# Attention and an ELU network on one core: the network's layers and the attention's values on float16 pairs

## The chip, the core and the metric

The kernel runs on one core of a Trainium2 chip. The core has five engines that take their instructions from queues of their own: TensorE (PE; its weight loads are listed apart as PEld), VectorE (DVE), ScalarE (ACT), GpSimd (POOL) and SyncE (SP, which here only issues DMAs). They share an on-chip memory of 128 partitions (SBUF); matmuls write to an accumulation memory (PSUM) of banks of 512 float32 values per partition. The metric is the time of one execution on the device in microseconds, the median of the runs.

## What is computed

Eight batches of eight heads, 576 positions, head size 64, then a network of 4608 tokens from 512 to 2048 to 512. The attention has a causal mask and a bias from running sums of `s`:

```python
scores = scale * np.matmul(q, k.transpose(0, 1, 3, 2))
cum = np.cumsum(np.maximum(s, 0.0), axis=-1)
bias = -(cum[:, :, :, None] - cum[:, :, None, :])
scores = np.where(causal, -1000000000.0, scores + np.minimum(bias, 0.0))
attn = np.exp(scores - np.max(scores, axis=-1, keepdims=True))
attn = attn / (np.sum(attn, axis=-1, keepdims=True) + 1e-09)
x = np.matmul(attn, v)                      # heads side by side: 4608 x 512
h = x @ w_in                                # 512 -> 2048
g = np.where(h > 0.0, h, np.exp(np.minimum(h, 0.0)) - 1.0)
out = (g @ w_out).astype(np.float32)        # 2048 -> 512
```

All inputs are float32 but the two weight matrices, which arrive as float64; the kernel takes them as pairs of 32-bit words and puts a float32 together on the chip. The output has to be near float32 accuracy, so most products are split into parts.

## The kernel before

**A planner sets the order.** The code describes operations (`op`) with a priority, what they read and write, and one or more "ways": an engine, an assumed cost, and the instruction. `Plan.issue` repeatedly picks the operation and the way that can start first by these assumed costs (ties go to the lower priority number) and writes it into its engine's queue. Each engine then runs its queue in that fixed order, and waits where an operand isn't there. Many vector operations can go to DVE, ACT or POOL (`rounded`, `rest`, `psum_copy`, `halved`); those that read PSUM can't go to POOL. DMAs go into SP's queue in the same way.

**Attention.** A batch has four pairs `j` of heads. The first 320 positions of batches 0 to 2 are done by twelve "low" units on whole float32 operands (`prepare_low`, `scoring_low`, `weighing_low`). Then batches 3 to 7 follow in full, and at the end the "late" rest (256 positions) of batches 0 to 2; that makes 40 whole and 24 late units of one head each (`Unit`, `prepare`, `scoring`, `weighing`), and 20 small units for the first 64 positions of a pair. A unit loads q and k, splits them in two parts each, multiplies the scores (L882), adds the mask and takes the minimum (L885), exponentiates (L890), and makes from each probability block a float16 high and low part (`halved`, L929 to L943). DMA transposes them (`turned_load`, L369) into `T`. `weighing` multiplies them by the values: `values` loads v as float32 and forms remainders (`rest`, L387 and L388), whose upper 16 bits serve as three bfloat16 parts of v. Each of five key blocks takes three matmuls (L1013), the last takes two: two parts of v side by side, against the high part of the probabilities; the same against the low part; and the third part of v. `halves` (L1092, L1097) adds the two halves of the result into `x`, which goes to DRAM (`x_dram`).

**The network** goes over 12 chunks of 384 tokens (`moe_chunk`), in the order in which attention delivers rows: chunk 0 has batch 0's low rows and 64 of batch 1, chunk 2 ends with rows of batch 3, chunk 8 with rows of batch 7, chunk 11 with late rows of batch 2. A chunk loads `x` (`load_x`), splits it into `xh` and `xl` (a float32 rounded for TensorE's fast float32 form, "fp32r" in the profile, and its remainder), and goes over 16 slices f of 128 hidden values: `hidden(f)` multiplies, for four blocks c, high by high, high by low and low by high (L1178, 12 matmuls of 384 columns); ACT takes the exponential (L1186), ACT or DVE the part below zero (L1191 or L1195), DVE joins (L1200), ACT or DVE rounds into `gh` (L394), DVE forms `gl` (L1203); `project(f)` multiplies three blocks of 128 tokens in three parts each (L1216, 9 matmuls of 512 columns). `project(f-1)` stands behind `hidden(f)` in the queue. Chunks alternate with attention on PE from chunk 0 on.

**The weights.** `load_weights` loads 32 units (16 slices, two matrices) of 512 KB into buffers `io` (two; at first also two of `xx`, where `xh` and `xl` come later). Each is turned from float64 words into float32 by one ACT and two DVE operations (L544, L547, L550), then split by `rounded` and `rest` (L376 to L388) into `w_in_f[f]` or `w_out_f[f]`, which stay for the whole run. Their priority is `W0 + WD * f`, with WD 5, so they come between the low units. Until its first 60 us are over, the planner fills PE with scratch transposes (L1267).

Of the kernel before, what the change touches and what calls it, by code (L numbers as in the profile page):

```python
# [17 lines left out]
P = 128  # L18
# [6 lines left out]
N_ST, N_A, N_AV, N_H, N_IO, N_G, N_X, N_T, N_K = 2, 2, 1, 2, 2, 1, 1, 2, 1  # L25
# [6 lines left out]
W0, WD = 45, 5  # L32
# [3 lines left out]
N_HOME = 0  # L36


NATIVE, WHOLE = 0, 0
# [13 lines left out]
class Buf:  # L53


    def __init__(self, pool, shape, dtype, name, tag=None, bufs=1, others=()):
# [4 lines left out]
        self.others = [((id(pool), o[0]), *o[1:]) for o in others]  # L61
        self.tile = None
        self.parts = {}
        self.users = 0
        self.until = 0.0

# [11 lines left out]
class Plan:  # L78
# [32 lines left out]

    def op(self, prio, ways, reads=(), writes=(), late=()):
# [5 lines left out]
        for accesses, write in ((reads, False), (writes, True)):  # L118
            for a in accesses:
                b, part = a if isinstance(a, tuple) else (a, None)  # L120
                if not b.parts and b not in o.bufs:

                    n = self.tags.get(b.key, 0)
                    self.tags[b.key] = n + 1
                    o.new.append((b, n))
                    b.first = o
# [34 lines left out]
    def issue(self):  # L161
# [19 lines left out]
        while pending:  # L181
# [10 lines left out]
            for o in pending:  # L192
                t = 0.0
                for b, k in o.new:
# [4 lines left out]
                    if b.others and not busy:  # L199
# [77 lines left out]
def pe4(n):  # L277

    return 4 * pe(n)

# [35 lines left out]
def kernel(  # L316
# [66 lines left out]

    def rest(prio, n, dst, src, hi, reads, writes, only=None):
# [28 lines left out]
    vs = [plan.buf(const, [P, NQ + 1, 4, D], F32, f"vs_{k}") for k in range(2)]  # L413
# [110 lines left out]
    w_in_f, w_out_f = ([plan.buf(sb, [P, 2, 512], F32R, f"{n}_{f}") for f in range(NF)] for n in ("wi", "wo"))  # L524
    homes = [b.key[1] for pair in zip(w_in_f, w_out_f) for b in pair]
    wide = w_in.dtype != F32

    urgent = []

    def load_unit(f, kind, src, parts):  # L530

        prio = W0 + WD * f
        a, n = src.shape[1], f"{kind}{f}"
        later = homes[max(homes.index(parts.key[1]) + 1, len(homes) - N_HOME) :]
        shape, dtype = ([P, 512, 2], U32) if wide else ([P, 512], F32)
        raw = plan.buf(sb, shape, dtype, f"w_{n}", tag="io", bufs=N_IO,
                       others=[("xx", 2, 0)] + [(t, 1, 0) for t in later])
        if wide:
            load(prio, lambda: raw.v.rearrange("p (a n) t -> p a (n t)", a=a),
# [11 lines left out]
                raw.v[:, :, 0], raw.v[:, :, 1], 3, raw.v[:, :, 0],  # L551
                ALU.logical_shift_left, ALU.bitwise_or))], [(raw, 1)], [(raw, 0)])
            words = (raw, 0)
# [5 lines left out]
        def value():  # L559
            return raw.v[:, :, 0].bitcast(F32) if wide else raw.v  # L560
# [807 lines left out]
```

## Time and profile before

| what | value |
|---|---|
| time, median of 3 runs (lowest, highest) | 1125.65 us (1124.69, 1129.84) |
| the profiled execution: span from first to last instruction | 1121.7 us |
| median time less that span | 4.0 us |
| mean granted clock of TensorE | 1.000 |
| first matmul of the network | 87.15 us |
| last attention result stored | 968.88 us |
| DMA, mean over the span | 140 GB/s |

The profile lists for each engine the time in which it had an instruction running. Matmuls overlap on PE: the next one starts while the last one drains, so their durations add up to more than the time they take, and the distance of two starts is what one costs. "Idle before" is the time in which the engine had nothing running before an instruction, with whoever ended it. A granted clock of 1.00 is TensorE at full speed.

### The profile page before, as it was taken

The numbers are of one execution on the slowest core, as the hardware profiler recorded it, in microseconds if no ns is written. First come the engines' busy times: TensorE is split into PE (matmuls) and PEld (weight loads), VectorE is DVE, ScalarE is ACT, GpSimd is POOL, SyncE is SP. The second block draws the span as 40 slices with busy tenths as digits, with TensorE's granted clock in tenths as the row PEclk, the third lists the DMA queues.
The fourth block names the chain that finished last, engine by engine and source line by source line (L and its number), as shares of the span: only waits on it lengthen the run. The fifth ranks groups of instructions, "written<-read, shape, count | busy, mean of one in ns | idle before, by whom it ended". The sixth has DMA issues, their size and how long they took to land.

```text
span 1121.7 us, 19900 instructions
## 1 busy us (share of the span) xinstructions
PE 1098.8 (98%) x6069; PEld 955.5 (85%) x6069; DVE 842.3 (75%) x2133; ACT 627.1 (56%) x1525; POOL 448.5 (40%) x657
## 2 busy tenths in 40 slices
PE   8999999999999999999999999999999999999998
PEld 7779888888888888888888888888888888899997
DVE  6888999778888887677887887788888888422322
ACT  5887666455556655555565555555655556433433
POOL 7663573345436234344333533445444433100000
PEclk9999999999999999999999999999999999999999
DMA  6976788567666855666755656667787687210000
GB/s 171 274 196 203 183 206 191 124 141 167 154 127 143 175 126 127 153 141 139 158 117 122 162 136 138 145 131 177 167 185 165 138 191 144 51 57 1 29 1 28
DMA packets 341689, 156.52 MB, mean 140 GB/s; under 512 B 266424, under 2 KB 320464, under 8 KB 341584
## 3 DMA queue, kind: packets, MB, share of 16 engines
q1 hardware_dynamic: 341584, 155.27, 59.4%
q8 instruction: 48, 0.79, 0.3%
q14 instruction: 57, 0.47, 0.1%
HBM read 79.66 MB, written 19.32 MB: 88 GB/s over the span
## 4 chain that ended last, share of the span: by engine, by line
PE 73%; DVE 4%; DMA 3%; issue 1%; POOL 1%; ACT 1%; SPq 1%; POOLq 0%; DVEq 0%; ACTq 0%
PE o L1216 29%; PE h L1178 29%; PE av L1013 8%; PE sc L882 6%; DVE p L943 1%; DMA T<-p 1%; DMA stq<-in_qT_dram 1%; DVE p L885 1%; DMA q<-qs 0%; DMA vs<-in_vb_dram 0%; DVE h L1200 0%; DVE xl L387 0%; DMA out_dram<-ost 0%; DMA x_dram<-x 0%; DVE qs L387 0%
## 5 line engine op out<-in xcount | busy, mean ns | idle before, releaser
L1178 PE MATMUL h<-xh,wi 128*128 128x384 f32 x1536 | 444.6, 339 | 1.1 <-DVE gl L1203 1.1
L1216 PE MATMUL o<-wo,gh 128*128 128x512 f32 x1152 | 362.1, 395 | 0.1
L1178 PEld LDWEIGHTS h<-xh,wi 128*128 128x128 f32 x1536 | 282.6, 188 | 9.3 <-DVE gl L1203 2.4
L1178 PE MATMUL h<-xl,wi 128*128 128x384 f32 x768 | 258.4, 336 | 0.0
L1216 PEld LDWEIGHTS o<-wo,gh 128*128 128x128 f32 x1152 | 207.0, 188 | 27.4 <-DVE mn L885 0.5
L1216 PE MATMUL o<-wo,gl 128*128 128x512 f32 x576 | 227.3, 395 | 0.9 <-DVE gl L1203 0.9
L1200 DVE SCALAR_TENSOR_TENSOR h<-h,g 128x384 f32<-128x384 f32 x192 | 107.8, 561 | 121.6 <-ACT g L1191 120.1
L1186 ACT ACTIVATE g<-h 128x384 f32<-128x384 f32 x192 | 94.1, 490 | 175.4 <-PE h L1178 166.0
L890 ACT ACTIVATE p<-p,mn 128x192 f32<-128x192 f32 (+1 forms) x232 | 144.9, 625 | 72.2 <-DVE mn L885 69.1
L943 DVE SCALAR_TENSOR_TENSOR p<-p,sm,p 128x512 f16<-128x512 f32 (+3 forms) x239 | 170.6, 741 | 8.1 <-POOL p L935 4.9
L1178 PEld LDWEIGHTS h<-xl,wi 128*128 128x128 f32 x768 | 144.4, 188 | 6.8
L935 POOL TENSOR_SCALAR p<-p,sm 128x512 f16<-128x512 f32 (+3 forms) x125 | 87.8, 709 | 134.8 <-DVE sm L896 51.8
L394 ACT CAST gh<-h 128x384 fp32r<-128x384 f32 x175 | 83.5, 477 | 86.7 <-DVE h L1200 85.4
L1203 DVE TENSOR_TENSOR gl<-h,gh 128x384 fp32r<-128x384 f32 x192 | 105.8, 551 | 32.8 <-ACT gh L394 31.7
L1216 PEld LDWEIGHTS o<-wo,gl 128*128 128x128 f32 x576 | 108.0, 188 | 25.2 <-DVE gl L1203 1.3
L885 DVE CUSTOM_DVE_ANT_0 p<-sc,maskw 128x192 f32<-128x192 f32 (+1 forms) x232 | 109.7, 482 | 24.9 <-PE sc L882 21.1
L1013 PEld LDWEIGHTS <-vs 128*128 128x128 bf16 x896 | 79.7, 98 | 49.7 <-issue 13.9
L1013 PE MATMUL av<-T,vs 128*128 128x256 f16 (+5 forms) x896 | 119.2, 285 | 2.8 <-DMA T<-p 2.1
L388 POOL TENSOR_TENSOR vs<-vs 128x320 f32<-128x320 f32 x72 | 60.4, 839 | 124.6 <-DMA vs<-in_vb_dram 71.1
L882 PE MATMUL sc<-kh,qs 128*128 128x192 f32 (+2 forms) x272 | 87.2, 325 | 2.1 <-DVE mn L885 1.8
L882 PE MATMUL sc<-k,q 128*128 128x192 f32 (+2 forms) x272 | 83.8, 312 | 1.4 <-POOL k L388 0.9
L1191 ACT ACTIVATE g<-g 128x384 f32<-128x384 f32 x138 | 72.5, 525 | 4.2
(149 smaller groups left out, 1368.7 us busy)
## 6 DMA issues: line engine op xcount, KB each, us to landing
stk<-in_kT_dram SPq DMA_DIRECT2D x64, 288.0 KB
vs<-in_vb_dram SPq DMA_DIRECT2D x64, 160.0 KB
stq<-in_qT_dram SPq DMA_DIRECT2D x40, 256.0 KB
w_i<-in_w_in_dram SPq DMA_DIRECT2D x16, 512.0 KB
w_o<-in_w_out_dram SPq DMA_DIRECT2D x16, 512.0 KB
out_dram<-ost SPq DMA_DIRECT2D x32, 256.0 KB
x_dram<-x_None SPq DMA_DIRECT2D x20, 288.0 KB
q<-qs SPq DMA_DIRECT2D x40, 128.0 KB
```

Source lines behind the costliest of these rows:

```text
L394: ("ACT", act_c(n), lambda: act.copy(dst(), src())),
L882: pe_.matmul(view(sc.v[:, :cw]), l, r, start=n == 0, stop=n == len(pairs) - 1)
L885: op(prio, [("DVE", 84 + dve_p(cw), lambda i=i, sc=sc: dve.tensor_tensor_reduce(pt.v[:, i * cw : (i + 1) * cw], sc.v[:, :cw], mv(i * cw, c ...
L890: op(prio, [("ACT", 480 + w / 1.2, lambda: act.activation(pt.v[:, :w], pt.v[:, :w], AF.Exp, bias=mn.v[:, n - 1 : n], scale=-1.0, accum_out ...
L935: ("Pool", 160 + 1.04 * n, lambda part=part: pool.tensor_scalar(part(t16, 0), own(part), sm.v[:, r], 1.0, ALU.mult, ALU.mult)),
L943: ("DVE-SB", dve_2(n), lambda part=part: dve.scalar_tensor_tensor(part(t16, 1), own(part), sm.v[:, r], part(t16, 0), ALU.mult, ALU.subtract)),
L1013: op(prio, [("PE", cost, lambda m=m, operands=operands, rows=rows: pe_.matmul(av.v[:rows, dst], *operands(), start=first and m == 0, stop= ...
L1178: pe_.matmul(hp.v[:, :TC], w_in_f[f].v[:, part, c * P : (c + 1) * P], xx.v[:, c, :TC], start=(c == 0 and m == 0), stop=(c == NCB - 1 and m ...
L1186: op(side, [("ACT", act_c(TC), lambda: act.activation(g.v[:, :TC], hp.v[:, :TC], AF.Exp))], [hp], [g])
L1200: op(side, [("DVE", dve_p(TC), lambda: dve.scalar_tensor_tensor(hp.v[:, :TC], hp.v[:, :TC], 0.0, g.v[:, :TC], ALU.max, join[0]))], [g], [hp])
L1203: op(side, [("DVE", dve_p(TC), lambda: dve.tensor_tensor(gl.v[:, :TC], hp.v[:, :TC], gh.v[:, :TC].bitcast(F32), ALU.subtract))], [hp, gh], ...
L1216: pe_.matmul(acc[i].v, g.v[:, tb], w_out_f[f].v[:, part], start=(f == 0 and m == 0), stop=(f == NF - 1 and m == 2),)
```

## The change

All of it concerns in what form operands stand, and what has to be known before they can be made.

- **The network's chunks 1 to 11** multiply float16 pairs: `x`, `w_in`, the hidden values and `w_out` are each a float16 high part and a float16 remainder, after scaling by a power of two. The number of matmuls is the same. `hidden` now joins by a maximum in PSUM (`g` times the scale against `h`), and the pair `gg` is formed with a factor `2**-DOWN`; the scale is undone on the way out (`output`).
- **Chunk 0** (384 tokens) multiplies `x` and the weights as whole float32 (`hidden_native`, `project` with `native`): one product in place of three, no split. Its `x` is loaded straight into the buffers that `xh` and `xl` take later.
- **Scales** are found on chip: `peak` reduces each weight unit, each low unit's values and each group's values to one largest magnitude per partition. `scales_of` reduces these to one column, stores it to DRAM, loads it back in all partitions, reduces again and turns the exponent into a power of two. `x` is scaled by the scale of the values it comes from, since an average of values is no larger than the largest.
- **The weights** are kept as float32 (`w_all`) at first, are split into `w_parts` once all 32 are loaded and reduced (`weight_scales`, `split_unit`), and only the float16 parts are used after chunk 0. WD goes from 5 to 3; raw weights have the two `io` buffers alone.
- **The attention's values** of the 64 whole and late units are a scaled float16 pair. `group_values` loads a batch's values at once (four loads, placed 60 priority steps ahead), into the place of `w_parts[3]` for the first batch and of `w_all` for later ones; `pair_values` splits them. A key block takes two matmuls, both parts of v side by side, against the high and the low part of the probabilities; the last takes one.
- `kh` gets two buffers instead of one.

```diff
-N_ST, N_A, N_AV, N_H, N_IO, N_G, N_X, N_T, N_K = 2, 2, 1, 2, 2, 1, 1, 2, 1
+N_ST, N_A, N_AV, N_H, N_IO, N_G, N_X, N_T, N_K, N_V = 2, 2, 1, 2, 2, 1, 1, 2, 2, 2
+V_AHEAD = 60
-W0, WD = 45, 5
+W0, WD = 45, 3
...
+    def peak(prio, n, src, reads, at, axis=mybir.AxisListType.X, aside=None, also=()):
+        col = slice(at, at + 1)
+        ways = [("DVE-SB", 100 + 1.04 * n, lambda: dve.tensor_reduce(
+            peaks.v[:, col], src(), axis, ALU.max, apply_absolute_value=True))]
+        if aside is not None:
+            ways.append(("ACT", 480 + n / 1.2, lambda: act.activation(
+                aside(), src(), AF.Abs, accum_out=peaks.v[:, col])))
+        op(prio, ways, reads, [(peaks, at), *also])
...
+    def scales_of(prio, spans, dst):
...
+        def largest():
+            for m, (at, k) in enumerate(spans):
+                dve.tensor_reduce(own.v[:, m : m + 1], peaks.v[:, at : at + k], mybir.AxisListType.X, ALU.max)
+        def exponents():
+            dve.tensor_reduce(own.v, every.v.rearrange("p (n q) -> p n q", q=P), mybir.AxisListType.X, ALU.max)
+            bits = own.v.bitcast(U32)
+            dve.tensor_scalar(bits, bits, 23, 23, ALU.logical_shift_right, ALU.logical_shift_left)
+            power(scales.v.bitcast(U32)[:, dst : dst + n], bits, 2 * 127 + TOP)
...
+        op(prio, [("DVE-SB", 30.0 + 70 * n, largest)], used, [own])
+        load(prio, lambda: aside.v.rearrange("n p -> p n"), lambda: own.v, [own], [aside], P * n * 4)
+        load(prio, lambda: every.v, lambda: aside.v.rearrange("n p -> (n p)").partition_broadcast(P),
+             [aside], [every], P * P * n * 4)
+        op(prio, [("DVE-SB", 300.0 + 130 * n, exponents)], [every], [own, (scales, dst)])
...
+    def split_unit(f, kind):
...
+        scaled(prio, 512, high_v, value, lambda: scales.v[:, col], [place, (scales, 0)], [high])
+        op(prio, [("DVE-SB", dve_2(512), lambda: dve.scalar_tensor_tensor(
+            low_v(), value(), scales.v[:, col], high_v(), ALU.mult, ALU.subtract))],
+           [place, (scales, 0), high], [low])
...
+    def group_values(u):
+        at = groups.index((u.b, u.blocks[0] > 0))
+        prio, first, col = u.prio - V_AHEAD, A_GROUP + at * (NP + 1), 4 + 2 * at
+        home = w_parts[NG - 1] if at == 0 else w_all[(at - 1) % NG]
+        va = plan.buf(sb, [P, NP, 2 * (NQ + 1), D], F32, f"va_{at}", tag=home.key[1])
+        for j in range(NP):
+            load(prio, lambda j=j: va.v[:, j], lambda j=j: vb[u.b, j, :, 1:], [], [(va, j)], P * 2 * (NQ + 1) * D * 4)
+            peak(prio, 2 * (NQ + 1) * D, lambda j=j: va.v[:, j], [(va, j)], first + j, mybir.AxisListType.XY)
+        scales_of(prio, [(first, NP + 1)], col)
...
+            def own():
+                return u.values.v[:, u.h, kb].rearrange("p a d -> p (a d)")
+            used = [(u.pt, i) for i in range(i0, last)] + [(u.values, (m, u.h)) for m in range(2)]
+            pairs = [(used, lambda m=m: (own(), part(m))) for m in range(1 + (kb < last))]
...
+        def hidden_native(f):
...
+            for c in range(NCB):
+                op(main, [("PE", pe4(TC), lambda c=c: pe_.matmul(
+                    hp.v[:, :TC], weight(f, 0)[1]()[:, c * P : (c + 1) * P], xc[c // 2].v[:, c % 2, :TC],
+                    start=c == 0, stop=c == NCB - 1))],
...
+            gg = parts[f] = plan.buf(sb, [P, 2, TMAX], F16, f"gg_{ch}_{f}", tag="gg", bufs=2)
+            op(side, [("DVE", dve_p(TC), lambda: dve.scalar_tensor_tensor(
+                hp.v[:, :TC], g.v[:, :TC], by(2 if sign[0] else 1), hp.v[:, :TC], ALU.mult, ALU.max))],
+               [g, cs], [hp])
...
+    weight_scales()
+    for f in range(NF):
+        split_unit(f, 0)
+        split_unit(f, 1)
```

426 lines of the change are left out of this document (241 added, 185 removed).

## The prediction

> **What bounds the kernel now.** The page comes first: what is busy, what the throttle granted, what the chain of waits is made of.
>
> ```profile
> span 1121.7 us, 19900 instructions
> ...
> PE 1098.8 (98%) x6069; PEld 955.5 (85%) x6069; DVE 842.3 (75%) x2133; ACT 627.1 (56%) x1525; POOL 448.5 (40%) x657
> ...
> PE 73%; DVE 4%; DMA 3%; issue 1%; POOL 1%; ACT 1%; SPq 1%; POOLq 0%; DVEq 0%; ACTq 0%
> ```
>
> TensorE is busy 98% of the span and makes 73% of the chain. But an average hides stages, so I asked for windows cut where the work changes: start, first chunk of the network, attention with the network, network alone.
>
> ```profile
> 0.00:87.00 87.00, 77.42 (x466) 64.55 (x467) 70.63 (x235) 64.53 (x207) 57.41 (x133) 1.00 0.82 216
> 87.00:180.00 93.00, 90.88 (x497) 80.26 (x494) 84.69 (x197) 64.24 (x149) 53.16 (x66) 1.00 0.74 192
> 180.00:968.00 788.00, 780.95 (x4362) 675.72 (x4363) 638.85 (x1619) 441.61 (x1058) 333.16 (x452) 1.00 0.66 148
> 968.00:1122.00 154.00, 149.57 (x749) 134.97 (x747) 48.14 (x85) 56.69 (x115) 4.80 (x6) 1.00 0.07 22
> ```
>
> Columns are the stage, its length, busy time of PE, PEld, DVE, ACT and POOL, granted clock, DMA share, GB/s. From 87 to 968 us PE idles 2.1 + 7.1 = 9.2 us in 881, at full clock. So time taken out of PE there shortens the run, as long as PE still finds operands. DVE, at 638.85 of 788 (81%), is next in line. The kernel therefore gains what its matmuls lose, less what the other engines can't deliver.
>
> **What a product costs now.** Busy times of overlapping matmuls can't be divided by their count; I take starts from the timeline. One round of a network slice f, in the stage without attention:
>
> ```profile
> 1027.47 0.33 PE L1178 MATMUL h<-xh,wi 128*128 128x384 f32 x1
> ...
> 1029.58 0.63 PE L1216 MATMUL o<-wo,gh 128*128 128x512 f32 x2
> ...
> 1031.66 0.33 PE L1178 MATMUL h<-xh,wi 128*128 128x384 f32 x1
> ```
>
> Twelve products of 384 columns take 2.11 us, nine of 512 take 2.08: 4.19 us a slice, 0.455 ns a column, 67 us a chunk. Float16 is already in the kernel: the attention's values product streams T in it (weights bfloat16).
>
> ```profile
> 170.68 2.10 PE L1013 MATMUL av<-T,vs 128*128 128x512 f16 x14
> 172.61 0.47 PE L1216 MATMUL o<-wo,gh 128*128 128x512 f32 x1
> ```
>
> A whole unit has 3 x (512+448+320+192) + 2 x 64 = 4544 columns, done in 172.61 - 170.68 = 1.93 us: 0.425 ns a column. A late unit has 3008 (256, 256, 256, 192, and 64 twice). Whole float32 operands stand in the scores of the low units:
>
> ```profile
> L882 PE MATMUL sc<-kl,ql 128*128 128x320 f32 x44 | 15.0, 434 | 0.0
> ...
> 84.96 0.70 PE L882 MATMUL sc<-kl,ql 128*128 128x320 f32 x2
> ```
>
> Eleven of the twelve units (the first keeps its keys under another name) make 22 such products and leave 44 records: two a product. Two records last 0.70 us and one 0.434, so the second starts 0.266 us after the first: 0.83 ns a column and record, 1.66 a product's column.
>
> **The change, part by part.** *Network in float16 pairs* (`hidden`, `project`), 11 of 12 chunks: still three products for one, 21 matmuls a slice, 9216 columns x 0.425 = 3.92 us instead of 4.19. 0.27 x 16 x 11 = **-47.5 us**. No row has a float16 stationary operand; the nearest, 512 columns against bfloat16, gives the 0.425. Its bounds are 0.455 (no gain) and 0.42 (-56).
>
> *Chunk 0 on whole float32* (`hidden_native`): 4 x 384 + 3 x 512 = 3072 columns x 1.66 = 5.1 us a slice, +0.91 x 16 = **+14.6 us**.
>
> *Values* (`own`, `products`): a key block takes two products instead of three, the last one instead of two. A whole unit falls to 3008 columns (-1536, -0.65 us), a late one to 1984 (-1024, -0.435). 40 x 0.65 + 24 x 0.435 = **-36.4 us**.
>
> PE's sum: -69.3 us.
>
> *Vector work.* Prices from these rows:
>
> ```profile
> L380 DVE TENSOR_SCALAR wo<-w_o 128x512 fp32r<-128x512 f32 x5 | 2.3, 457 | 0.1
> L550 DVE SCALAR_TENSOR_TENSOR w_o<-w_o 128x512 uint32<-128x512 uint32 x16 | 12.2, 766 | 0.0
> L387 DVE TENSOR_TENSOR wo<-w_o,wo 128x512 fp32r<-128x512 f32 x15 | 11.4, 760 | 0.1
> L387 DVE TENSOR_TENSOR vs<-vs 128x320 f32<-128x320 f32 x56 | 29.7, 530 | 8.4 <-DMA vs<-in_vb_dram 5.4 <-POOL vs L388 2.7
> L1203 DVE TENSOR_TENSOR gl<-h,gh 128x384 fp32r<-128x384 f32 x192 | 105.8, 551 | 32.8 <-ACT gh L394 31.7
> L895 DVE TENSOR_SCALAR sm<-sm 128x4 f32<-128x4 f32 x40 | 8.2, 204 | 4.5 <-ACT p L890 3.9
> ```
>
> Largest-magnitude reductions are new: 32 of 512 elements (weights), 32 of 640 (value groups), 12 of 448 (low units). No row has one. By the one-operand row (0.457 us for 512) they cost 14.6 + 17.6 + 4.9 = 37 us, by the two-operand row (0.766) 24.5 + 29.8 + 8.2 = 62. I take 62, the end that speaks against the change; ACT may take part of the weights'. The Trainium skill, "VectorE: DVE Perf Modes", section "The perf-mode tier table (the rule you actually need)", gives a reduction only the one-element rate, whatever the type; by it the dearer end holds, by the cheaper row PE would have 25 us more cover from DVE. No run here shows a reduction yet.
>
> The rest is small. Nine scale groups and eleven `chunk_scales` are some 130 tiny operations at 0.204 us: +27. Weights' low parts now on DVE alone, 32 x 0.77 against 11.4 for `wo` and some 9 for `wi` (the same rate): +4. Values, 64 low parts of 0.53 in place of 29.7 (POOL loses its share): +5 at most. Chunk 0 drops 16 `gl` (0.551) and four roundings: -12. DVE's sum is +86; with a part of the weights' reductions on ACT I take **+75**, between 50 and 86. It lies beside PE and costs the end nothing while DVE keeps up. What it costs if not is the first rival. The exponential and `halves` with a scale from a column, `gg` in place of `gh`/`gl`: same operations, same counts, costed at nothing; between the last of these steps and the product that reads it the timeline leaves room:
>
> ```profile
> 1027.84 0.56 DVE L1203 TENSOR_TENSOR gl<-h,gh 128x384 fp32r<-128x384 f32 x1 [0.54 <-ACT gh L394]
> ```
>
> `gl` is done at 1028.40, its product starts at 1029.58: 1.18 us of slack, of which a shorter slice takes 0.27.
>
> *The added wait.* Scales go through DRAM: a store and a load on SP, one behind the other, nine times. A load that a computation awaits takes about 2.66 us here, issue to use:
>
> ```profile
> 75.81 0.32 SPq L364 DMA_DIRECT2D xc<-x_dram  x1
> ...
> 78.47 0.51 POOL L376 TENSOR_SCALAR xh<-xc 128x384 fp32r<-128x384 f32 x1 [0.62 <-DMA xc<-x_dram]
> ```
>
> Two of these and DVE's steps are some 7 us a group. Behind the second, all of SP's later issues stand (attention's loads, transposes, outputs), at most 2.7 us a time. Eight groups are asked for well ahead of their attention; I cost them at nothing. Values' loads keep their bytes. The ninth, for the weights, gates chunk 1. Its cover is chunk 0:
>
> ```profile
> 87.15 0.42 PE L1178 MATMUL h<-xh,wi 128*128 128x384 f32 x1
> ...
> 158.81 0.53 SPq L364 DMA_DIRECT2D w_o<-in_w_out_dram  x1
> ```
>
> The last weight is issued at 158.81; landing, conversion, reduction, scales and first split end near 175. Chunk 0 starts near 87 and has 16 x 5.1 = 82 us of PE at some 0.85 of it: it ends near 184. Nothing shows, by 9 us; if the cover is gone, each microsecond costs about 0.74, the network's 67 of each chunk's 90 (the ends of chunks 1 and 7 below are 6 x 90.1 us apart).
>
> *What is late next.* Each chunk waits for its attention. Last `x` store, then the end of the chunk before it (chunks 2, 8, 11):
>
> ```profile
> 246.32 0.35 SPq L364 DMA_DIRECT2D x_dram<-x_None  x1
> 264.05 0.52 SPq L364 DMA_DIRECT2D out_dram<-ost  x1
> ...
> 766.34 0.35 SPq L364 DMA_DIRECT2D x_dram<-x_None  x1
> 804.70 0.35 SPq L364 DMA_DIRECT2D out_dram<-ost  x1
> ...
> 968.88 0.34 SPq L364 DMA_DIRECT2D x_dram<-x  x1
> 1052.13 0.34 SPq L364 DMA_DIRECT2D out_dram<-ost  x1
> ```
>
> Leads are 18, 38 and 83 us. A chunk shrinks from some 90 to 82 us, the first grows by 15: chunk 2 would start near 272, chunk 8 near 770, chunk 11 near 1000. Attention at its present pace just makes it, but with 75 us more on DVE. The row of 87 to 180 shows DVE at 84.69 of 93 (91%) with PE idle 2.3%, against 0.9% at 81%. I price this at PE idling 2% instead of 1% of 900 us: **+10**, from 0 to +40.
>
> Sum: 1121.7 - 69.3 + 10 = 1062.4 in span. The median of the times, 1125.65, is 4 us above the profiled span; with that, **1066 us**. Own range 1046 to 1086.
>
> **Rivals.** *DVE sets the pace.* Up to 968 us DVE works 70.6 + 84.7 + 638.9 = 794 us, 82%. With 75 more it has 869 before the last chunk, which needs 63 us and 8 for ends and launch: time = 869/share + 71. My forecast needs 87%; at 85% it is 1093, at 82% 1131, all gone. For: list order at such a load leaves holes, as 81% so far shows. Against: 91% from 87 to 180, and ACT and POOL, with 39 and 58% of 180 to 968 free, can take the operations that have several engines. 1086 to 1120.
>
> *The scales' barrier is late (slower than before).* Chunk 1 can't begin until all 32 weights have passed two `io` buffers, been reduced and come back. At 0.74 a microsecond the 59 us of gain are gone when this ends 80 us after chunk 0, at 264, and it is 0.5% slower from 272 us. For: only two buffers now, no overflow into `xx`. Against: `x` of chunk 0 no longer occupies them, and 158.81 would have to become some 255. Price 1131 to 1150. In a sentence of its own: the Trainium skill, "TensorE: Matmul & The Clock Gate", section "What's actually happening", halves the clock after an idle window of about 3.4 us, which would make such a hole dearer; every stage here shows 1.00, so no run shows it.
>
> *The change doesn't shorten the network's products.* Float16 against float16 stationary stays at 4.19 us a slice: -36.4 + 14.6, with the 10, leaves about 1114.
>
> **How the numbers follow.** A measurement of this kernel tells about 0.5% from no change: below 1120 is faster, above 1131 slower. Forecast 0.67; DVE 0.18; no shorter products 0.04; late barrier 0.07; one of the first two ending within 0.5% of no change, 0.04. Faster 0.67 + 0.18 + 0.04 = 0.89, same 0.04, slower 0.07. For eight in ten I take 1046 to 1110: the forecast's own range (0.67) and, of DVE's, the part up to 1110 (24 of its 34 us, 0.13). The favourable bound of the network's price (-56) lies in it, and DVE down to a share of 84%; no gain at all in the network's products (1114) lies outside, with its 0.04.
>
> **What would show it.** Tail slices of 3.9 us; chunk 0 at 5.1 us of PE a slice; av groups of 9 matmuls in 1.28 us; PE idle from chunk 0 on near 18 us; no hole at the start of chunks 1, 2 and 8; clock 1.00. Wrong if DVE's share stays near 82% with PE idle over 30 us, if reductions exceed 1 us, or if the clock falls with float16 streaming.

## The result: no faster, and where the time went

The changed kernel takes 1139.67 us (median of four runs, 1134.56 to 1141.69) against 1127.38 us of the kernel before on the same chip (four runs; the 1125.65 above is the median of three of them): a ratio of 1.0104, interval 1.0069 to 1.0140. The forecast was 1066 us, in a range of 1046 to 1110. The kernel became about 1% slower.

The page of the profiled execution (span and instructions; busy time of each engine; the chain that ended last):

```profile
span 1137.9 us, 19124 instructions
...
PE 1052.2 (92%) x5650; PEld 618.8 (54%) x5650; DVE 897.2 (79%) x2250; ACT 651.3 (57%) x1513; POOL 509.0 (45%) x756
...
PE 30%; DVE 4%; DMA 1%; issue 1%; ACT 1%; POOL 1%; POOLq 0%; DVEq 0%; SPq 0%; ACTq 0%
```

TensorE lost 46.6 us of busy time, and the span grew by 16.2: its idle time went from 1121.7 - 1098.8 = 22.9 to 85.7 us. The same stages as before, in the view by windows (stage, length, busy time of PE, PEld, DVE, ACT and POOL, granted clock, DMA share, GB/s):

```profile
0.00:87.00 87.00, 72.65 (x430) 61.12 (x431) 65.48 (x217) 56.66 (x182) 42.57 (x110) 0.96 0.76 195
87.00:180.00 93.00, 89.33 (x340) 53.44 (x339) 81.66 (x215) 64.20 (x162) 37.39 (x59) 0.98 0.81 214
180.00:968.00 788.00, 724.37 (x3968) 414.11 (x3967) 666.48 (x1650) 450.82 (x1015) 404.37 (x551) 0.98 0.63 142
968.00:1137.90 169.90, 165.84 (x918) 90.10 (x916) 83.54 (x171) 79.62 (x156) 24.70 (x37) 1.00 0.20 48
```

Two things are new. In the long stage PE idles 63.6 of 788 us, where it idled 7.1. And the granted clock, 1.00 in every stage before, is 0.96 to 0.98 up to 968 us. The mean over the span is 0.981, which is 2 x 0.019 x 1137.9 = 43 us at half clock. By windows laid on these stretches PE is busy in 39.4 of them; work done at half clock takes about twice as long (six products L1341 last 2.78 us at 374.85, at half clock, and 1.47 at 642.63), so some 20 us of PE's busy time are only slow.

The matmuls themselves do what was forecast. Two rounds of the last chunk, by starts in the timeline:

```profile
1100.61 0.33 PE L1304 MATMUL h<-xh,wp 128*128 128x384 f16 x1
...
1102.56 2.11 PE L1341 MATMUL o<-wp,gg 128*128 128x512 f16 x9
...
1104.50 0.33 PE L1304 MATMUL h<-xh,wp 128*128 128x384 f16 x1
```

A slice is 1104.50 - 1100.61 = 3.89 us (forecast 3.92, before 4.19). The account closes within 3 us: 1098.8 - 69.3 (the forecast's sum for PE) = 1029.5 us of matmuls, + 20 for half clock, + 85.7 idle = 1135, where the span is 1138.

So the question is where 63 us of idle time and the half clock come from. One of the new ways through DRAM (`own` stored to `aside`, `aside` loaded to `every`), in the timeline:

```profile
643.90 0.37 SPq L378 DMA_DIRECT2D aside<-own  x1
...
650.92 0.33 SPq L378 DMA_DIRECT2D every<-aside  x1
...
652.63 0.33 PE L1304 MATMUL h<-xh,wp 128*128 128x384 f16 x1
...
656.51 0.29 DVE L596 TENSOR_REDUCE own<-every 128x1 f32<-128x128 f32 x1 [6.43 <-DMA every<-aside]
...
657.20 0.62 DVE L1313 SCALAR_TENSOR_TENSOR h<-g,cs,h 128x384 f32<-128x384 f32 x1
...
659.32 0.55 DVE L1322 SCALAR_TENSOR_TENSOR gg<-h,gg 128x384 f16<-128x384 f32 x1
659.92 0.48 PE L1304 MATMUL h<-xh,wp 128*128 128x384 f16 x1 [6.97 <-DVE gg L1322]
```

Read from the bottom: PE stood 6.97 us for `gg`, which DVE could not make because its queue stood 6.43 us at the reduction of `every`. That load was issued 7.0 us after the store, since it must wait for the store to land, and took 5.6 more. All nine are not alike; the view of waits gives the sums (us, times, longest), the second row for SP's queue:

```profile
DVE own L596 <- DMA every<-aside: 18.0, 5, 6.4
...
SPq L378 <- DMA aside<-own: 33.1, 7, 6.8
```

And what the transfers do meanwhile, by windows:

```profile
640.00:646.00 6.00, 5.90 (x33) 3.34 (x32) 5.50 (x16) 2.85 (x9) 1.61 (x3) 1.00 0.68 138
646.00:656.00 10.00, 6.96 (x43) 4.36 (x42) 2.99 (x10) 4.27 (x9) 3.12 (x7) 1.00 0.06 20
656.00:660.00 4.00, 0.08 (x1) 0.08 (x1) 3.39 (x9) 2.12 (x5) 1.00 (x1) 0.74 0.69 225
```

For ten microseconds behind the store nearly nothing moves: 20 GB/s, where the span's mean is 138. For about half of that time SP stands and issues nothing, so this row alone does not tell whether the store slows other transfers.

### The profile page after: what moved, and what is told of

Read it like the earlier page. It is cut to its first block, busy times and chain, and to the rows that moved or that the text cites. A ratio compares the mean times of both kernels' runs of the same rounds, so it can differ in the third digit from the quotient of the medians.

```text
span 1137.9 us, 19124 instructions
## 1 busy us (share of the span) xinstructions
PE 1052.2 (92%) x5650; PEld 618.8 (54%) x5650; DVE 897.2 (79%) x2250; ACT 651.3 (57%) x1513; POOL 509.0 (45%) x756
## 5 line engine op out<-in xcount | busy, mean ns | idle before, releaser
L1304 PE MATMUL h<-xh,wp 128*128 128x384 f16 x1408 | 394.1, 328 | 25.1 <-DVE gg L1322 24.9
L1341 PE MATMUL o<-wp,gg 128*128 128x512 f16 x1584 | 394.9, 386 | 2.3 <-DVE gg L1319 1.8
L1304 PEld LDWEIGHTS <-wp 128*128 128x128 f16 x2112 | 195.9, 98 | 176.5 <-issue 41.0
L1341 PEld LDWEIGHTS <-gg 128*128 128x128 f16 x1584 | 148.1, 99 | 160.7 <-issue 11.7
L1304 PE MATMUL h<-xl,wp 128*128 128x384 f16 x704 | 230.5, 327 | 3.8 <-POOL xl L1254 3.7
L1268 ACT ACTIVATE g<-h,cs 128x384 f32<-128x384 f32 x176 | 101.9, 579 | 142.1 <-PE h L1304 140.0
L1313 DVE SCALAR_TENSOR_TENSOR h<-g,cs,h 128x384 f32<-128x384 f32 x176 | 108.5, 617 | 77.9 <-ACT g L1275 76.6
L1017 POOL TENSOR_SCALAR p<-p,sm 128x64 f16<-128x64 f32 (+3 forms) x130 | 88.0, 683 | 94.9 <-DVE sm L978 57.4
L967 DVE CUSTOM_DVE_ANT_0 p<-sc,maskw 128x192 f32<-128x192 f32 (+1 forms) x232 | 108.9, 480 | 16.2 <-PE sc L964 13.7
L1322 DVE SCALAR_TENSOR_TENSOR gg<-h,gg 128x384 f16<-128x384 f32 x176 | 97.0, 551 | 19.3 <-ACT gg L1317 17.2
L1084 PE MATMUL av<-T,v 128*128 128x256 f16 (+5 forms) x576 | 84.0, 292 | 2.2 <-DMA T<-p 2.2
L1084 PEld LDWEIGHTS <-v 128*128 128x128 f16 x576 | 55.7, 99 | 40.1 <-issue 7.8
```

What stands on the lines that cost most here:

```text
L967: op(prio, [("DVE", 84 + dve_p(cw), lambda i=i, sc=sc: dve.tensor_tensor_reduce(pt.v[:, i * cw : (i + 1) * cw], sc.v[:, :cw], mv(i * cw, c ...
L1017: ("Pool", 160 + 1.04 * n, lambda part=part: pool.tensor_scalar(part(t16, 0), own(part), sm.v[:, r], 1.0, ALU.mult, ALU.mult)),
L1084: op(prio, [("PE", cost, lambda m=m, operands=operands: pe_.matmul(av.v[:, dst], *operands(), start=first and m == 0, stop=last and m == l ...
L1268: op(side, [("ACT", act_c(TC) + (0 if native else 90), lambda: act.activation(g.v[:, :TC], hp.v[:, :TC], AF.Exp, scale=1.0 if native else ...
L1304: pe_.matmul(hp.v[:, :TC], weight_part(f, 0, part)[1]()[:, c * P : (c + 1) * P], xx.v[:, c, :TC], start=(c == 0 and m == 0), stop=(c == NC ...
L1313: op(side, [("DVE", dve_p(TC), lambda: dve.scalar_tensor_tensor(hp.v[:, :TC], g.v[:, :TC], by(2 if sign[0] else 1), hp.v[:, :TC], ALU.mult ...
```

## The experiments

A "way" from here on is one way through DRAM, a store and a load back (not the planner's ways of doing an operation). **Theory 1**: engines stand behind the nine ways (SP's queue for the store, DVE for the load). **Theory 2**: DVE, 55 us fuller, doesn't keep up, and the ways matter little. Ratios are to the kernel before, on the same chip.

**Take the ways out, tell the planner, lighten DVE, put ways into the old kernel.** Four edits; e1 takes a constant for the maximum over partitions, e3 reduces eight elements of each unit, the ways of e4 carry nothing that is used:

```diff
e1_no_trip
-            dve.tensor_reduce(own.v, every.v.rearrange("p (n q) -> p n q", q=P), ...)
+            dve.tensor_reduce(own.v, bound.v[:, : n * P].rearrange("p (n q) -> p n q", q=P), ...)
-        load(prio, lambda: aside.v ...)
-        load(prio, lambda: every.v ...)
e2_told
-        load(prio, lambda: aside.v ..., P * n * 4)
+        load(prio, lambda: aside.v ..., P * n * 4, lag=7200.0)
-             [aside], [every], P * P * n * 4)
+             [aside], [every], P * P * n * 4, lag=5000.0)
e3_small
-            peaks.v[:, col], src(), axis, ALU.max, apply_absolute_value=True))]
+            spare.v[:, col], few(src()), axis, ALU.max, apply_absolute_value=True))]
e4_before_trips
+        op(prio, [("DVE-SB", 100.0, lambda: dve.tensor_reduce(
+            own.v, u.qs.v[:, :5].bitcast(F32), mybir.AxisListType.X, ALU.max))], [(u.qs, 0)], [own])
+        load(prio, lambda: aside.v.rearrange("n p -> p n"), lambda: own.v, [own], [aside], P * 4)
+        load(prio, lambda: every.v, lambda: aside.v[:, :112]....partition_broadcast(P), [aside], [every], P * P * 4)
+        op(prio, [("DVE-SB", 430.0, exponents)], [every], [own])
```

> The changed kernel without the way through DRAM: the nine scale groups take their exponent from a constant tile (0.5 in all places, which bounds the data) instead of storing one column and loading it back in all partitions. All reductions and all small operations on DVE stay; what is left out is the maximum over the partitions. Theory 1 (the store and the load take some 7 and 5 us, SP and DVE stand behind them, PE runs dry and its clock is halved afterwards): the idle holes next to the nine groups (35 us of them) and most of the half clock go, 1080 to 1100 us, mean clock above 0.99. Theory 2 (DVE is too full with the new reductions, the holes only happen to lie there): within 10 us of the changed kernel, 1130 or more.

> The changed kernel with the same instructions, but the planner is told that the store of a scale column lands 7.2 us after its issue and the load 5.0 us (it assumed 1.8 for both), so that it places what waits for them later. Theory 1: most of the gain of the run without the way through DRAM, 1085 to 1110 us, and SP's waits for the store nearly gone. Theory 2: within 10 us of the changed kernel. If only the bare latency of the weights' scales counts, also no change.

> The changed kernel with its 76 reductions to the largest magnitude cut to 8 elements each (they take some 0.15 us instead of 0.5 to 0.8, all on DVE; the scale then comes from a constant 0.5; the magnitudes of the data are left out). The way through DRAM stays with all its waits. Theory 2: DVE loses some 45 us of work, the holes shrink, at least 25 us faster than the changed kernel. Theory 1: DVE's load isn't what makes the holes, within 10 us of the changed kernel (1130 to 1145), clock still near 0.98.

> The kernel before, with eight ways through DRAM added, one at the start of each batch of the attention: a small reduction on DVE, the store of one column, the load back in all partitions, a reduction of what came back; nobody uses the result. Theory 1: SP and DVE stand behind each, 3 to 5 us of PE are lost at most of the eight, and the clock is halved after some: 20 to 45 us slower than before (1146 to 1171). Theory 2: eight times half a microsecond of DVE, within 5 us of before.

| run | median us | ratio, interval |
|---|---|---|
| e1_no_trip | 1091.70 | 0.9714, 0.9677 to 0.9750 |
| e2_told | 1144.31 | 1.0176, 1.0128 to 1.0224 |
| e3_small | 1157.61 | 1.0292, 1.0264 to 1.0320 |
| e4_before_trips | 1191.16 | 1.0593, 1.0559 to 1.0628 |

Without the ways the change gains nearly 3%. Lighter reductions gain nothing, which speaks against theory 2; e3 is even 18 us slower than the changed kernel, in a new order of the planner, and no run shows why. Telling the planner how long a way takes gained nothing either. And eight idle ways cost the old kernel 65 us, more than theory 1 expected (20 to 45): nearly as much as the waits of SP for the stores (43.5 us) and of DVE for the loads (20.0) in its trace together, as if each fell on PE in full. Theory 1 had the place right and not yet the mechanism.

**Another route for the scales, and a second suspect.** In e2's trace SP hardly waits for the stores any more (5.9 us in three places), and the largest hole in PE (23 us at 215 us) lies beside this, in the timeline of DVE:

```profile
213.45 18.97 DVE L650 SCALAR_TENSOR_TENSOR wp<-wa,scales,wp 128x512 f16<-128x512 f32 x27
```

Low parts of 27 weights stand in a row, ahead of what attention needs. **Theory 3**: this block hides the gain of e2. e6, e7 and e8 space the split three slices ahead in chunk 1, with the ways over TensorE, told, and as they are. e5 replaces the way: TensorE transposes the column, repeated, into PSUM, so that each partition has all 128 values; the scales are the same. It also puts the weights' scales and split just before the last slice of chunk 0, and the planner finds a new order for it.

```diff
e5_turned
-        load(prio, lambda: aside.v ...)
-        load(prio, lambda: every.v ...)
+        def turn():
+            for m in range(n):
+                pe_.transpose(every.v[:, m * P : (m + 1) * P], own.v[:, m : m + 1].to_broadcast([P, P]), ident)
+        op(prio, [("PE", 111.0 * n, turn)], [own], [every])
e6_turned_spread, e7_told_spread, e8_spread
-    for f in range(NF):
-        split_unit(f, 0)
-        split_unit(f, 1)
...
+                for kind in range(2):
+                    split_unit(f + 3, kind, [plan.ops[first]])
```

> The changed kernel with every way through DRAM replaced: TensorE turns the column (one transpose of the column repeated 128 times, into a PSUM bank), DVE reduces what stands there. Scales are found from the data as in the change. The weights' group uses one of the two banks of the hidden values and stands just before the last slice of chunk 0. Theory 1 (the way through DRAM): as the run without it, 1085 to 1105 us. Theory 2 (DVE too full): within 10 us of the changed kernel, near 1140. Were it only that the scale was a constant there, also near 1140.

> As the run before, and the split of the weights is paced: slice f + 3 is split once the hidden layer of slice f of chunk 1 has begun, instead of all 64 operations at once as soon as the scales are known. Theory 3 (the block of low parts on DVE, 27 one behind the other in the run with the told planner, starves PE between chunks 0 and 1): 5 to 15 us faster than the run before, 1075 to 1095, and no hole over 3 us between 180 and 260 us. If the block doesn't matter when the scales come early: within 5 us of the run before.

> The changed kernel with the planner told the landing times (7.2 and 5.0 us) and the weights' split paced as above. In the run with the told planner alone the hole of 23 us at 215 us stood where DVE did 27 low parts in a row. Theory 3: that hole goes with its half clock, 25 to 40 us faster than that run: 1105 to 1120. If telling the planner doesn't help in itself: near 1140.

> The changed kernel with the paced split alone, the way through DRAM as it was. Theory 1 holds the groups' ways for the larger part: at most 10 us faster than the changed kernel, 1130 to 1142. If the block of splits were the main cause: 1100 or less.

| run | median us | ratio, interval |
|---|---|---|
| e5_turned | 1096.62 | 0.9731, 0.9717 to 0.9746 |
| e6_turned_spread | 1102.46 | 0.9779, 0.9763 to 0.9796 |
| e7_told_spread | 1142.74 | 1.0134, 1.0087 to 1.0181 |
| e8_spread | 1158.62 | 1.0276, 1.0253 to 1.0298 |

e5 does all of the computation and is faster than both kernels. Theory 3 falls: with the block spaced, e7's 23-us hole is gone and the time is not, and e6 is no faster than e5. Waits told in advance still cost; that a wait is unplanned can't be what they cost by. e8, the spaced split alone, is 19 us slower than the changed kernel, against what was expected, and no run shows why.

**Halves of a way.** The old kernel with eight stores alone (e9), with stores and loads that DVE doesn't read (e10), both cut from e4; and e5 with e3's reductions (e11).

```diff
e9_stores (against e4)
-        load(prio, lambda: every.v ...)
-        op(prio, [("DVE-SB", 430.0, exponents)], [every], [own])
e10_no_reader (against e4)
-        op(prio, [("DVE-SB", 430.0, exponents)], [every], [own])
```

> The kernel before with the first half of the idle ways alone: eight times a DVE reduction to one column (as in the run with the idle ways) and its store of 128 single values to DRAM; no load, nothing waits for the store. If what costs is engines and queues that stand behind a wait (SP's queue for the store, DVE for the load), nothing is left here but eight short reductions of some 0.15 us: 0 to +5 us, ratio 1.000 to 1.005. If the store itself is in the way of other transfers (128 packets of 4 bytes ahead of them in the rings), most of the +65 us is here: +30 to +65, ratio 1.03 to 1.06.

> As the run before it, and the load that spreads the values to all partitions, which SP issues when the store has landed; DVE does not read what it brings. SP's queue stands some 5 us in each of eight places (40.8 us over seven waits in the run with the idle ways), DVE does not stand. If SP's standing queue is the cost, nearly all of the +65 us is here: +40 to +65, ratio 1.035 to 1.058. If it is DVE's wait, +5 to +20, ratio 1.005 to 1.018, and the rest came with the reader.

> The kernel with the way over TensorE in place of the way through DRAM, and its 76 reductions cut to eight elements (leaves out the maxima over the rest; the trips and all waits stay): DVE loses some 45 us of 890. That kernel still has 54.6 us of TensorE idle and 29.2 at half clock against 22.9 and 0 before. If the rest is DVE's fuller load, idle falls to 25 to 40 us and the time to 1070 to 1085 us, ratio 0.95 to 0.963; if the rest has another cause (the order of work, waits at the seams), nothing within 8 us of 1096.6.

| run | median us | ratio, interval |
|---|---|---|
| e9_stores | 1187.85 | 1.0546, 1.0521 to 1.0570 |
| e10_no_reader | 1188.98 | 1.0561, 1.0535 to 1.0588 |
| e11_turned_small | 1101.75 | 0.9779, 0.9756 to 0.9803 |

Eight stores that nobody waits for cost 61 us. Either the store itself is in the way of other transfers, or a new entry in the planner's list changes the whole order for the worse: e9's order of matmuls differs from the old kernel's from the 621st of 6069 on. **Theory 4** is this order. e11 has 31 us less work on DVE than e5 and gains nothing.

**Hold the order still.** e12 and e13 keep every instruction of the changed kernel in its place: e12 doesn't issue the eighteen transfers, e13 issues them but DVE reads a constant. e14 gives the old kernel's planner only the eight reductions. e15 puts the ways into the old kernel when its instructions are written out, behind the planner's back.

```diff
e12_after_order
-        load(prio, lambda: aside.v ...)
-        load(prio, lambda: every.v ...)
+        op(prio, [("SP", SP_COST, lambda: None, LAG, P * n * 4)], [own], [aside])
+        op(prio, [("SP", SP_COST, lambda: None, LAG, P * P * n * 4)], [aside], [every])
e12_after_order, e13_unread
-            dve.tensor_reduce(own.v, every.v.rearrange("p (n q) -> p n q", q=P), ...)
+            dve.tensor_reduce(own.v, bound.v[:, : n * P].rearrange("p (n q) -> p n q", q=P), ...)
e15_before_order
+            while engine == "DVE" and self.due and start >= self.due[0][0]:
+                self.due.pop(0)[1]()
             trace()
...
+        def out():
+            dve.tensor_reduce(own.v, ident[:, :5], mybir.AxisListType.X, ALU.max)
+            nc.sync.dma_start(aside.v.rearrange("n p -> p n"), own.v)
+            nc.sync.dma_start(every.v, aside.v[:, :112].rearrange("n p -> (n p)").partition_broadcast(P))
+        def back():
+            dve.tensor_reduce(own.v, every.v, mybir.AxisListType.X, ALU.max)
```

(In e13 the exponent is worked out in a tile of its own, `most`, so that DVE needn't wait until `own` has been stored.)

> The changed kernel with every instruction in the order that its planner found, and only the eighteen transfers of the nine ways through DRAM left out (DVE's reduction reads a constant tile; leaves out the maximum over partitions). If engines that stand behind the ways are the cost, the time falls as without the ways in the plan (1091.7): 1090 to 1105 us, ratio 0.968 to 0.98. If the order is the cost, which the planner found differently because the ways were in its list, it stays at 1125 to 1140 us, ratio 1.00 to 1.012, with the holes at 186, 420 and 544 us still there.

> The changed kernel in its own order with all eighteen transfers issued, but DVE reads the constant tile, not what the load brings (the maximum over partitions is left out): SP's queue stands behind the stores, DVE behind nothing. If SP's queue is what costs, the time is that of the changed kernel, 1130 to 1140 us; if DVE's wait is, that of the run without the transfers, whatever that gives; between the two in the share of each.

> The kernel before with the eight DVE reductions to one column alone (0.15 us each, nothing reads them), planned like the rest: no store, no load. If the 61 us of the run with the stores come from the stores, this gives the time before within 3 us, ratio 0.997 to 1.003. If they come from the planner's order, which any new entry shifts, this loses as much as the shift of order gives: +5 to +60 us, ratio 1.005 to 1.053.

> The kernel before with every instruction in the order of its own plan, and eight idle ways (reduction, store, load, reduction of what it brings) put in behind the planner's back, the reader 4 us after the first in the plan's time. If engines that stand behind the ways are the cost: SP stands some 7 us and DVE some 6 to 8 us in eight places, +25 to +65 us, ratio 1.022 to 1.058. If the order is the cost, +0 to +12 us, ratio 1.00 to 1.011.

| run | median us | ratio, interval |
|---|---|---|
| e12_after_order | 1093.83 | 0.9707, 0.9673 to 0.9740 |
| e13_unread | 1122.64 | 0.9961, 0.9941 to 0.9981 |
| e14_reductions | 1129.51 | 1.0034, 1.0014 to 1.0054 |
| e15_before_order | 1209.08 | 1.0733, 1.0706 to 1.0760 |

Theory 4 falls. In the very order of the changed kernel, the time without the transfers is that of e1. Of the 46 us between (1139.67 - 1093.83), 29 come with the transfers and SP's wait for the stores (e13 keeps it), and 17 with DVE's wait for what they bring. e14's order is shifted too, though only from the 4871st matmul on, and loses 3 us. In the old order, eight ways cost 83 us, more than was expected (25 to 65); the view of waits of e15:

```profile
DVE own L1119 <- DMA every<-aside: 68.8, 8, 12.4
...
SPq L1116 <- DMA aside<-own: 55.7, 8, 8.4
```

A store is waited for 55.7 / 8 = 7.0 us in the mean.

**Why a store of 512 bytes is so slow.** It is 128 single values of 4 bytes, one from each partition. e16 is e15 with one row of 512 bytes from one partition instead; e17 is e15 with the column's store alone, for which nothing waits; e18 is the changed kernel in its own order with rows for columns. The rows of e16 and e18 are constants, so these stores do not wait for DVE's reduction to one column; in e15 that wait was 4.4 us in four places, in the changed kernel 4.2 in three. SP's wait for the store and DVE's for the load stay.

```diff
e16_row (against e15)
-            nc.sync.dma_start(aside.v.rearrange("n p -> p n"), own.v)
+            nc.sync.dma_start(aside.v, ident[:1, :])
e17_stores_order (against e15)
-            nc.sync.dma_start(every.v, aside.v[:, :112].rearrange("n p -> (n p)").partition_broadcast(P))
-        def back():
-            dve.tensor_reduce(own.v, every.v, mybir.AxisListType.X, ALU.max)
e18_after_row (against the changed kernel)
-        load(prio, lambda: aside.v.rearrange("n p -> p n"), lambda: own.v, [own], [aside], P * n * 4)
+        load(prio, lambda: aside.v.rearrange("(o n) p -> o (n p)", o=1), lambda: bound.v[:1, : n * P],
+             [own], [aside], P * n * 4)
```

> The kernel before in the order of its own plan with the eight idle ways put in behind it, but the store is one row of 512 bytes from one partition in place of 128 single values from 128 partitions; the load, SP's wait for the store and DVE's wait for the load stay. If the single values are what makes the store slow to land (6 to 8 us), it lands in some 2 to 3 us, as other loads and stores do, and the cost falls from +83 to +20 to +45 us, ratio 1.018 to 1.04. If every store to DRAM that is waited for costs this, it stays at +70 to +90 us, ratio 1.06 to 1.08.

> The kernel before in the order of its own plan with the eight reductions and stores of 128 single values alone: no load, nothing waits for the store. If the store holds up the transfers behind it (in the run with the stores alone in a new plan, packets of 2304 bytes took 845 ns in the 7 us behind one store, where their median is 93), the loss is most of that run's 61 us: +40 to +65 us, ratio 1.035 to 1.058. If that run lost by its order, +0 to +10 us, ratio 1.00 to 1.009.

> The changed kernel in its own order with all eighteen transfers and all waits (SP's for the store, DVE's for the load), but each store is one row of 512 or 1536 bytes of a constant tile in place of the column of single values (leaves out the maximum over partitions). If the column's shape is the cost, nearly all of the 46 us that fell away without the transfers falls away here too: 1092 to 1106 us, ratio 0.97 to 0.982. If the waits cost whatever the shape, 1120 to 1140 us.

| run | median us | ratio, interval |
|---|---|---|
| e16_row | 1139.34 | 1.0131, 1.0098 to 1.0164 |
| e17_stores_order | 1167.97 | 1.0374, 1.0350 to 1.0399 |
| e18_after_row | 1096.17 | 0.9714, 0.9672 to 0.9755 |

The shape decides. As rows the eight ways cost the old kernel 14 us instead of 83 (20 to 45 were expected), with SP still waiting for each store and DVE for the loads; in the view of waits of e16 the store is now awaited 14.4 / 8 = 1.8 us:

```profile
DVE own L1119 <- DMA every<-aside: 13.1, 7, 3.2
...
SPq L1116 <- DMA aside<-ident: 14.4, 8, 2.4
```

And the columns alone, awaited by nobody, cost 42. They hold up what is behind them. The first store of e15 is issued at 97.79, of e16 at 99.64, of e17 at 97.81; the same 5 us by windows, in the kernel before, with the column and its waits (e15), with the row (e16), and with the column alone (e17):

```profile
100.80:105.80 5.00, 5.00 (x27) 4.47 (x26) 4.48 (x8) 2.85 (x6) 1.77 (x2) 1.00 0.76 232
```

```profile
100.80:105.80 5.00, 0.93 (x6) 0.61 (x4) 0.02 (x1) 1.01 (x2) 2.05 (x3) 0.95 0.00 0
```

```profile
100.80:105.80 5.00, 2.99 (x17) 2.54 (x16) 2.73 (x7) 2.32 (x5) 2.87 (x4) 1.00 0.53 147
```

```profile
100.80:105.80 5.00, 5.00 (x28) 4.61 (x27) 2.85 (x5) 1.50 (x3) 2.82 (x3) 1.00 0.69 39
```

The last columns are DMA share and GB/s: 232, 0, 147, 39. In e15 nothing moves, since SP stands. In e17 SP goes on issuing, the transfers' time is taken (0.69), and a sixth of the bytes arrives. What this does to a weight unit behind the store, in the timelines of the kernel before and of e17:

```profile
97.21 0.50 SPq L364 DMA_DIRECT2D w_o<-in_w_out_dram  x1
...
102.46 0.47 DVE L547 TENSOR_SCALAR w_o<-w_o 128x512 uint32<-128x512 uint32 x1
```

```profile
99.16 0.38 SPq L370 DMA_DIRECT2D w_o<-in_w_out_dram  x1
...
108.50 0.43 DVE L553 TENSOR_SCALAR w_o<-w_o 128x512 uint32<-128x512 uint32 x1 [4.78 <-DMA w_o<-in_w_out_dram]
```

9.3 us from issue to use instead of 5.3, and DVE stands in front of all that it has queued. The packets of this column are not what takes the time: in the trace of e17 its 4-byte packets last 0.015 us at most, and they are over by 100 us. The 4096-byte packets of the weight unit behind them last up to 6.1 us, where the longest of this size in the kernel before is 1.6.

e18 closes the case in the changed kernel itself: rows for columns, and 1139.67 becomes 1096.17, within 2.3 us of no transfers at all. Its view of waits, where the changed kernel had 18.0 and 33.1 us:

```profile
DVE own L601 <- DMA every<-aside: 3.3, 2, 2.1
...
SPq L378 <- DMA aside<-bound: 1.7, 2, 1.1
```

The rival that every store that is waited for costs this would have kept it at 1120 or more.

## Why the prediction was wrong, step by step

**PE's sum of -69.3 us: right.** 1052.2 less 20 for half clock is 1032, against 1029.5.

**The added wait: the step that failed.** I took "a load that a computation awaits takes about 2.66 us" for store and load alike, and costed eight groups at nothing. That row is a load of rows to 128 partitions. No row of the kernel before shows a store of single values to DRAM, and where no row shows an operation its cost wants a bound from both sides; I gave it none above 2.7. SP waits 7.0 us for it, the load behind it takes 5 to 6, and it slows transfers that have nothing to do with it. I had named what stands behind the wait, "all of SP's later issues", and still priced it "at most 2.7 us a time". This term is worth 44 us, 1139.67 - 1096.17 (clock losses among them). With it the forecast would have been 1110; the next step and the clock make up the rest.

**PE idle +10, from 0 to +40: too small, within its bounds without the ways.** The whole rise is 62.8 us. Without the transfers, in the same order, idle is 1092.4 - 1038.1 = 54.3 us, by the page of e12:

```profile
span 1092.4 us, 19083 instructions
...
PE 1038.1 (95%) x5650; PEld 613.4 (56%) x5650; DVE 898.4 (82%) x2250; ACT 650.9 (60%) x1513; POOL 509.3 (47%) x757
```

That is +31. Whether a fuller DVE makes it is open. For it: in the view of waits of e12, PE's waits for DVE add up to 30 us, against 6 before, and the largest of them is for `gg`:

```profile
PE h L1308 <- DVE gg L1326: 18.5, 14, 5.8
```

Against it: 31 us less work on DVE (e11 against e5) did not shorten the run, in an order of its own. With 31 in place of 10, and the 7 us of clock losses below, 1066 becomes 1094; e12 measured 1093.83. That is inside the range of 1046 to 1110, but outside the forecast's own, which ended at 1086.

**DVE's +75 us, 50 to 86: in range.** It is 897.2 - 842.3 = 54.9. ACT took 17 of the weights' 32 reductions. The rest, by line and form:

```profile
L574 DVE TENSOR_REDUCE peaks<-va 128x1 f32<-128x640 f32 x32 | 25.4, 806 | 0.0
L574 DVE TENSOR_REDUCE peaks<-wa 128x1 f32<-128x512 f32 x15 | 10.2, 677 | 0.1
```

I had taken the dear end, 0.766 us per 512; measured 0.677, nearer to it than to 0.457.

**The clock: not in the sum.** I wrote that every stage shows 1.00 and left half clock to one rival. It costs 20 us in the changed kernel and 7 in e12 (half of the 14.8 us that PE works at half clock), a quarter to a third on top of the added idle time (62.8 and 31). Two places in the changed kernel by windows, each with the window before the half clock and the half clock itself:

```profile
371.20:374.60 3.40, 1.58 (x6) 0.65 (x7) 3.27 (x12) 2.35 (x8) 0.00 (x0) 1.00 1.03 207
374.60:378.00 3.40, 3.40 (x10) 1.48 (x11) 3.14 (x14) 1.78 (x7) 1.47 (x3) 0.50 1.02 292
654.50:657.90 3.40, 0.00 (x0) 0.00 (x0) 1.29 (x5) 0.04 (x1) 0.00 (x0) 1.00 0.72 254
657.90:664.70 6.80, 4.78 (x13) 1.75 (x13) 6.27 (x15) 4.02 (x10) 2.46 (x3) 0.50 0.63 138
```

After 3.4 us without work the clock is 0.50 for 6.8 us; after 3.4 us in which PE worked 1.58 it is 0.50 too, for 3.4. The Trainium skill, "TensorE: Matmul & The Clock Gate", section "What's actually happening", puts the halving after an idle window of about 3.4 us. The first pair agrees (0.50 after 3.4 us without work); the second shows that the window needn't be idle throughout.

**The rivals.** DVE sets the pace: its sign, a share near 82% with PE idle over 30 us, came true in e12 (82%, 54.3), whose time lies in this rival's 1086 to 1120; that DVE's load is the cause is not shown, as above. The scales' barrier late: the kernel did get slower, as this rival had it, but not by its mechanism. Scales for the weights were there at 197 us, and chunk 0, which I had ending near 184, ended at 214.6; the first product of chunk 1 starts at 214.4. Chunk 0 had its 82 us of PE at 0.58 of the time from 72.2 to 214.6, not at 0.85; PE was at work meanwhile, 93.33 of the 97 us from 87 to 184. No shorter float16 products: refuted by 3.89 us a slice.

## What to carry to other kernels

A value per partition that every partition needs should not go through DRAM as a column of single values: turn it first (TensorE does it in e5, for 43 us less). Stored as a row it is cheap too, but the rows tried here (e16, e18) were constants; real values would have to be brought into one partition first, and no run shows that price. When a change adds a transfer, price it by a row of the same shape and direction, and price too what it does to the transfers issued behind it; if no row shows that shape, its upper bound is open. And where a planner writes the order, a cause can be tested cleanly by putting the instruction into an order that is held fixed.

## What was not expected of the hardware

SP waits 7.0 us for a store of 128 x 4 bytes and 1.8 for one of 512 bytes from a single partition (e15, e16, means of eight); behind the column, other transfers move 39 GB/s where they moved 232, with nothing waiting for it (e17). The Trainium skill, "DMA: Bandwidth & Descriptors", section "Specifications", asks for at least 512 bytes a transfer for full rate and says that below it a read-modify-write is done. These two stores lie on its two sides as it says; the read-modify-write itself no run shows. The runs show besides that the price falls on neighbours. Why the column holds them up was not tried further.

The granted clock halves after one 3.4-us window in which TensorE was busy for less than about half of the time. I laid the windows on the grid of the clock's own changes, in the 17 of the 20 traces that have stretches of half clock before the end. Of the windows at full clock, 133 were followed by half clock; their busy share was 0 to 0.65, and 0.54 or less in all but three. The other 5260 had 0.40 to 1.00. So below 0.39 the clock was always halved, and between 0.40 and 0.65 sometimes. No long gap is needed: the longest in the stretch from 371.2 us is 1.8 us.
